# Distinct TensorE row groups for ScalarE's score sets, and a planner that serialises score matmuls sharing one

## The chip, the cores and the metric

The kernel runs on one core of a Trainium2 chip. The core has TensorE (PE in the profile; its weight loads are PEld), ScalarE (ACT), VectorE (DVE), GpSimd (POOL) and SyncE (SP), which issues the DMAs. The metric is the device time of one execution in microseconds.

## What is computed

The input x is 2048 tokens of 512 numbers. Four residual layers follow one another, A, B, A, B. A is softmax attention with 32 heads of 16 numbers that all share one key and one value head; B is linear attention with 32 heads of 16.

```python
def _A_ref(x, wq, wk, wv, wo):
    ...
    k = x @ wk
    v = x @ wv
    scores = jnp.einsum("bhqd,bkd->bhqk", q, k) * (Dh ** -0.5)
    p = _softmax(scores, axis=-1)
    o = jnp.einsum("bhqk,bkd->bhqd", p, v)
    return o.transpose(0, 2, 1, 3).reshape(B, S, H * Dh) @ wo
...
def _B_ref(x, wqkv, wo):
    ...
    pq, pk = phi(q), phi(k)
    kv = jnp.einsum("bhsd,bhse->bhde", pk, v)
    z = jnp.einsum("bhsd->bhd", pk)
    num = jnp.einsum("bhqd,bhde->bhqe", pq, kv)
    den = jnp.einsum("bhqd,bhd->bhq", pq, z)[..., None] + 1e-6
    return (num / den).transpose(0, 2, 1, 3).reshape(B, S, D) @ wo
...
x = x + _A_ref(_layernorm(x, axis=-1), A_wq, A_wk, A_wv, A_wo)
x = x + _B_ref(_layernorm(x, axis=-1), B_wqkv, B_wo)
x = x + _A_ref(_layernorm(x, axis=-1), A_wq, A_wk, A_wv, A_wo)
x = x + _B_ref(_layernorm(x, axis=-1), B_wqkv, B_wo)
```

## The kernel before

**The tiles.** An attention layer is cut into 32 units of 64 positions. A position is one score tile: 128 keys by 512 columns (queries of one or more heads). Its matmul contracts over 32 rows of TensorE's array (line 1035), and `parts` names which: position j of a unit uses row group i = j % 4, so neighbouring positions go 0, 1, 2, 3, 0, and so on. Matmuls in different row groups can run side by side.

**Two ways to the exponential.** A tile's exponential is made in one of two ways. ScalarE takes a *set* of three tiles (banks 0 to 2) or of two (banks 3 and 4) and turns it in one activation (line 1192) into PTA, of which there are five buffers. VectorE takes single tiles from banks 5 and 6: a first pass (line 1252, "P1" in the code) writes the exponential's bits as 16-bit whole numbers; three shifted copies per four tiles follow, on VectorE (line 1323) or in pieces on GpSimd (line 1313). The four versions are weighted in the PV matmuls, so a tile of VectorE's costs four PV matmuls and one of ScalarE's costs one. All PV matmuls (line 1072) go to 32 columns of the array each and add up in bank 7, which belongs to one unit at a time: when the unit is through, the bank is copied out (line 1084) and the next unit's PV matmuls may begin.

**The order.** No order is written out. When the program is built, `Sched` plays the kernel through with a clock of its own: every operation has a list of engines, a duration, a priority (a smaller number goes first) and buffers to acquire; whenever an engine is free, the first ready operation by priority is put on it. The order so found becomes the static instruction order of each engine, and only the waits between engines are left to the chip. TensorE has three modes in this model, scores ("S"), PV and column-tiled projections ("P"), and full-array matmuls ("F"); `pe_need` charges SWITCH between modes and keeps matmuls of one group apart. PASS, 0.217, is the planner's time of one pass. Some thirty knobs, such as HOLD, LEAD, BK, AP and the priorities PX and EVP, are changed every 6 us of the planner's clock by the table PLAN.

**Picking.** `step` (lines 1105 on) fills a free set: it walks from the first open position `pa` and takes the next positions that are not taken and whose keys and queries are ready. `fill` adds the score matmul, the exp and the PV matmuls of the set. Right after it, `dstep` picks a tile for VectorE LEAD positions ahead, in a row group that the set doesn't use where there is one. Positions that VectorE has taken are holes in what ScalarE's sets find later.

**The handover between layers.** `b_tile` finishes layer B for one token tile and prepares the next attention layer's; its operations carry priorities `pr`, from 1.0 upwards with the tile's number, as do those of `a_ready`. `layer_norm` is called with the same slope.

**Ports.** An operation with `port=True` on VectorE isn't started by the planner while GpSimd is at work, nor GpSimd's while such an operation runs (`_try`).

Of the kernel before, what the change touches and what calls it, by code (L numbers as in the profile page):

```python
# [20 lines left out]
LX = 0.338  # L21
HOLD = 0.836
# [36 lines left out]
YDT = 4  # L59
WT = 20.0  # L60
# [12 lines left out]
    (0.0, {'LX': 0.338, 'HOLD': 0.836, 'LEAD': 16, 'LEAD2': 14, 'NT0': 3, 'DMIN': 1, 'MP': 1, 'AP': 0.771, 'MF': 0.285, 'AF': 2.905, 'PCONT': 0.992, 'PX': 2.788, 'EVP': 1.5, 'EVX': 1.016, 'PQP': 1.6, 'PB': 1.6, 'PY': 4.497, 'PKV': 4.5, 'PTR': 2.887, 'PQL': 3.988, 'PHL': 3.855, 'PZ': 0.131, 'BK': 2.611, 'BKX': 0.376, 'BKR': 0.5, 'NPX': 6, 'PXP': 1.839, 'PXM': 0.376, 'PXA': 3.319}),  # L73
    (6.0, {'MF': 0.758, 'PX': 0.523, 'EVP': 0.969, 'PQP': 3.044, 'PTR': 1.57, 'PXM': 0.55, 'PXA': 4.0}),
    (12.0, {'EVP': 1.5, 'EVX': 1.666, 'PY': 3.366, 'PXM': 0.658}),
    (18.0, {'LX': 0.165, 'LEAD2': 15, 'NT0': 5, 'AP': 1.43, 'PX': 1.03, 'EVP': 0.969, 'EVX': 1.016, 'PY': 4.497, 'PXM': 0.55}),
    (24.0, {}),
    (30.0, {}),
    (36.0, {}),
    (42.0, {}),  # L80
    (48.0, {'PXM': 0.477}),
    (54.0, {'PKV': 3.114, 'PXM': 0.55, 'PXA': 3.298}),
    (60.0, {'LX': 0, 'MF': 0.453, 'EVP': 1.3, 'PQP': 2.524, 'PKV': 4.5, 'BKR': 0.271, 'PXM': 0.509, 'PXA': 4.0}),
    (66.0, {'HOLD': 0.625, 'LEAD2': 13, 'PQP': 2.757, 'PQL': 4.333, 'PXM': 0.51, 'PXA': 3.279}),
    (72.0, {'LX': 0.165, 'HOLD': 0.836, 'LEAD2': 15, 'AP': 2.013, 'MF': 0.758, 'EVP': 0.969, 'PQP': 3.044, 'PQL': 3.988, 'BKR': 0.5, 'PXM': 0.477, 'PXA': 4.0}),
    (78.0, {}),
    (84.0, {'AP': 0.235, 'EVX': 0.926, 'PQL': 4.305, 'BKR': 0.06, 'NPX': 5, 'PXM': 0.55}),
    (90.0, {'AF': 0.264, 'EVP': 0.5, 'PB': 1.661}),
    (96.0, {'AP': 1.43, 'AF': 2.905, 'PCONT': 0.519, 'EVP': 0.637, 'EVX': 1.016, 'PB': 1.6, 'PKV': 3.114, 'PQL': 4.602, 'BKR': 0.5, 'NPX': 6, 'PXA': 5.495}),
    (102.0, {'LX': 0.299, 'LEAD2': 14, 'PCONT': 0.64, 'BK': 5.514}),  # L90
    (108.0, {'LX': 0.165, 'LEAD2': 15, 'AP': 2.013, 'PCONT': 0.992, 'EVP': 1.815, 'PQP': 3.261, 'PKV': 4.5, 'PQL': 3.988, 'BK': 2.611, 'PXM': 0.477, 'PXA': 4.0}),
    (114.0, {}),
    (120.0, {'DMIN': 2}),
    (126.0, {'DMIN': 1, 'MP': 7, 'AP': 0.235, 'AF': 0.264, 'EVP': 0.5, 'EVX': 0.926, 'PQP': 3.044, 'PB': 1.661, 'PQL': 4.305, 'BKR': 0.06, 'NPX': 5, 'PXM': 0.55}),
    (132.0, {'LEAD2': 14, 'NT0': 3, 'DMIN': 2, 'MP': 1, 'AF': 2.905, 'EVP': 0.969, 'PB': 1.6, 'BKX': 1.173}),
    (138.0, {'HOLD': 0.825, 'NPX': 4, 'PXM': 0.32}),
    (144.0, {'HOLD': 0.836, 'LEAD2': 15, 'NT0': 5, 'AP': 2.013, 'AF': 2.795, 'EVP': 1.815, 'EVX': 1.173, 'PQP': 3.261, 'PQL': 3.988, 'BK': 3.918, 'BKX': 0.376, 'BKR': 0.5, 'NPX': 6, 'PXM': 0.477}),
    (150.0, {'AP': 0.738, 'BK': 0.896}),
    (156.0, {'HOLD': 0.651}),
    (162.0, {'PX': 3.422, 'PTR': 0.919}),  # L100
    (168.0, {'HOLD': 0.836, 'MP': 3, 'AP': 2.035, 'MF': 0.722, 'PCONT': 1.248, 'PX': 1.03, 'PQP': 1.861, 'PY': 4.5, 'PTR': 1.57, 'BK': 3.918}),
    (174.0, {'BKR': 1.227, 'PXM': 0.29}),
    (180.0, {'MP': 2, 'PCONT': 1.789, 'PQP': 3.771, 'PY': 1.858, 'PXP': 2.121, 'PXA': 3.431}),
    (186.0, {'DMIN': 1, 'EVP': 2.0}),
    (192.0, {'HOLD': 0.641, 'DMIN': 2}),
    (198.0, {}),
    (204.0, {'LEAD': 18, 'NPX': 1}),
    (210.0, {'LEAD': 16, 'EVP': 1.273, 'PTR': 1.665, 'PZ': 0.1, 'NPX': 6, 'PXP': 1.498}),
    (216.0, {'MP': 1, 'AF': 0.584, 'EVP': 2.0, 'PTR': 1.57, 'PZ': 0.131, 'BKX': 0.186, 'PXP': 2.121}),
    (222.0, {'LEAD': 18, 'AP': 1.138, 'PX': 1.994, 'PQL': 3.517}),  # L110
    (228.0, {}),
    (234.0, {'PKV': 3.786, 'PXA': 4.241}),
    (240.0, {'LX': 0.338, 'HOLD': 0.836, 'LEAD': 16, 'LEAD2': 14, 'NT0': 4, 'DMIN': 1, 'AP': 0.771, 'MF': 0.758, 'AF': 2.905, 'PCONT': 0.992, 'PX': 0.523, 'EVP': 1.5, 'EVX': 1.016, 'PQP': 3.287, 'PY': 4.497, 'PKV': 4.5, 'PQL': 3.988, 'BK': 2.611, 'BKX': 0.376, 'BKR': 0.5, 'PXP': 1.839, 'PXM': 0.645, 'PXA': 4.0}),
    (246.0, {}),
    (252.0, {}),
    (258.0, {'LEAD': 17, 'PB': 1.821, 'PTR': 1.458, 'PHL': 2.076, 'NPX': 9}),
    (264.0, {}),
    (270.0, {'LX': 0.165, 'HOLD': 0.641, 'LEAD': 18, 'LEAD2': 15, 'NT0': 5, 'DMIN': 2, 'AP': 2.993, 'MF': 0.722, 'AF': 0.584, 'PCONT': 1.789, 'PX': 1.994, 'EVP': 2.0, 'EVX': 0.948, 'PQP': 3.771, 'PB': 1.6, 'PY': 1.858, 'PKV': 3.297, 'PTR': 1.57, 'PQL': 3.517, 'PHL': 3.855, 'BK': 3.918, 'BKX': 0.186, 'BKR': 1.227, 'NPX': 6, 'PXP': 2.121, 'PXM': 0.29, 'PXA': 4.241}),
    (276.0, {}),
    (282.0, {'LX': 0.338, 'HOLD': 0.836, 'LEAD': 16, 'LEAD2': 14, 'NT0': 4, 'DMIN': 1, 'AP': 0.771, 'MF': 0.758, 'AF': 2.905, 'PCONT': 0.992, 'PX': 0.523, 'EVP': 1.5, 'EVX': 1.016, 'PQP': 3.287, 'PY': 4.497, 'PKV': 3.022, 'PQL': 3.988, 'BK': 1.481, 'BKX': 0.686, 'BKR': 0.5, 'PXP': 1.839, 'PXM': 0.645, 'PXA': 4.0}),  # L120
    (288.0, {'NT0': 3, 'DMIN': 2, 'MP': 2, 'EVX': 2.307, 'PQP': 3.044, 'PY': 4.5, 'PKV': 4.5, 'BK': 2.611, 'BKX': 0.376, 'PXM': 0.55}),
    (294.0, {}),
    (300.0, {'MP': 1, 'MF': 0.675, 'AF': 2.071, 'EVX': 1.496, 'PY': 4.497, 'BKX': 0.863, 'BKR': 0.871}),
    (306.0, {'LX': 0.321, 'HOLD': 0.641, 'LEAD': 18, 'LEAD2': 15, 'NT0': 5, 'AP': 2.993, 'MF': 0.722, 'AF': 0.584, 'PCONT': 1.789, 'PX': 1.994, 'EVP': 2.0, 'EVX': 0.948, 'PQP': 3.771, 'PY': 1.858, 'PKV': 3.297, 'PQL': 3.517, 'BK': 3.918, 'BKX': 0.186, 'BKR': 1.227, 'PXP': 2.121, 'PXM': 0.29, 'PXA': 4.241}),
    (312.0, {'LX': 0.331, 'HOLD': 0.48, 'LEAD2': 24, 'EVX': 1.448, 'PZ': 0.16}),
    (318.0, {'HOLD': 0.507, 'PXA': 3.973}),
    (324.0, {'EVX': 2.238, 'PXA': 1.205}),
    (330.0, {'LX': 0.321, 'HOLD': 0.641, 'LEAD2': 15, 'DMIN': 1, 'PX': 1.201, 'EVX': 0.948, 'PQL': 2.158, 'PHL': 1.07, 'PZ': 0.1, 'PXM': 0.298, 'PXA': 4.241}),
    (336.0, {'MF': 0.51, 'PCONT': 0.63, 'BKX': 0.274, 'PXP': 3.076}),
    (342.0, {'NT0': 3, 'EVP': 2.297, 'PTR': 1.732, 'PZ': 0.546, 'BKR': 1.5, 'PXM': 0.385}),  # L130
    (348.0, {'MF': 0.184}),
    (354.0, {}),
    (360.0, {'NT0': 5, 'MF': 0.722, 'PCONT': 1.789, 'EVP': 1.821, 'EVX': 0.573, 'PTR': 1.57, 'PZ': 0.1, 'BKX': 0.186, 'BKR': 1.227, 'PXP': 2.121, 'PXM': 0.298, 'PXA': 5.082}),
    (366.0, {'NT0': 2, 'PX': 3.845}),
    (372.0, {'LX': 0.338, 'HOLD': 0.836, 'LEAD': 16, 'LEAD2': 14, 'NT0': 3, 'AP': 0.771, 'MF': 0.758, 'AF': 2.905, 'PCONT': 0.992, 'PX': 0.523, 'EVP': 1.5, 'EVX': 1.016, 'PQP': 3.044, 'PY': 4.497, 'PKV': 4.5, 'PTR': 2.242, 'PQL': 3.988, 'PHL': 3.855, 'PZ': 0.131, 'BK': 2.611, 'BKX': 0.376, 'BKR': 0.5, 'PXP': 1.839, 'PXM': 0.355, 'PXA': 3.748}),
    (378.0, {'LEAD': 15, 'PB': 1.926, 'NPX': 4}),
    (384.0, {'NT0': 5, 'AF': 2.802, 'EVX': 2.838, 'PB': 1.6, 'BKR': 0.361, 'PXM': 0.364}),
    (390.0, {}),
    (396.0, {'DMIN': 2, 'AP': 1.529, 'PX': 3.842, 'PHL': 0.984, 'PXP': 0.75}),
    (402.0, {}),  # L140
    (408.0, {'EVP': 1.664, 'PQP': 3.211, 'NPX': 1}),
    (414.0, {'LEAD2': 15, 'PTR': 0.969, 'PQL': 1.195, 'NPX': 2, 'PXP': 1.756}),
    (420.0, {'EVX': 1.801, 'PQL': 1.84, 'PHL': 1.27, 'PXA': 2.587}),
    (426.0, {'HOLD': 0.841, 'LEAD2': 13, 'PY': 3.549, 'BKX': 0.607}),
    (432.0, {}),
    (438.0, {}),
    (444.0, {}),
    (450.0, {'HOLD': 0.836, 'LEAD2': 9, 'NT0': 3, 'DMIN': 1, 'AP': 0.771, 'AF': 2.905, 'PX': 0.523, 'EVP': 1.5, 'EVX': 1.589, 'PQP': 3.044, 'PY': 4.497, 'PTR': 1.313, 'PQL': 3.988, 'PHL': 3.855, 'BK': 2.321, 'BKX': 0.376, 'BKR': 0.5, 'NPX': 6, 'PXP': 1.839, 'PXM': 0.55, 'PXA': 4.0}),
# [6 lines left out]
    (492.0, {}),  # L155
    (498.0, {}),
    (504.0, {}),
    (510.0, {'LEAD': 12, 'EVX': 1.95, 'PQL': 3.343, 'BKX': 0.579}),
    (516.0, {}),
    (522.0, {}),  # L160
    (528.0, {}),
# [1497 lines left out]
```

## Time and profile before

| what | value |
|---|---|
| median of 3 runs (range) | 1495.05 us (1494.92 to 1497.63) |
| the profiled execution | 1498.8 us |
| its span | 1497.1 us |
| PE busy | 1459.2 us (97%), 16245 matmuls |
| ACT busy | 1444.9 us (97%), 1426 instructions |
| DVE busy | 1376.5 us (92%), 2433 instructions |
| POOL busy | 853.2 us (57%), 1360 instructions |
| exps of the first attention layer | 13.4 to 713.2 us |
| exps of the second attention layer | 749.7 us to 1456.2 us (start of the last) |

Every sum below is made against the span of the profiled execution. A busy PE is not PE at its peak, since several small matmuls can share the array at once. In the rows of groups, the part behind the first bar is the busy time in microseconds and the mean of one instruction in nanoseconds; behind the second bar stands how long the engine had been idle just before them, and what ended that idle time. In a row of the timeline stand the start, the length, the engine, the line and how many instructions were merged.

### The profile page before, as it was taken

The numbers are of one execution on the slowest core, as the hardware profiler recorded it, in microseconds if no ns is written. First come the engines' busy times: TensorE is split into PE (matmuls) and PEld (weight loads), VectorE is DVE, ScalarE is ACT, GpSimd is POOL, SyncE is SP. The second block draws the span as 40 slices with busy tenths as digits, with TensorE's granted clock in tenths as the row PEclk, the third lists the DMA queues.
The fourth block names the chain that finished last, engine by engine and source line by source line (L and its number), as shares of the span: only waits on it lengthen the run. The fifth ranks groups of instructions, "written<-read, shape, count | busy, mean of one in ns | idle before, by whom it ended". The sixth has DMA issues, their size and how long they took to land.

```text
span 1497.1 us, 38261 instructions
## 1 busy us (share of the span) xinstructions
PE 1459.2 (97%) x16245; PEld 492.0 (33%) x16255; DVE 1376.5 (92%) x2433; ACT 1444.9 (97%) x1426; POOL 853.2 (57%) x1360
## 2 busy tenths in 40 slices
PE   7999999999999999999899999999999999999998
PEld 4322333322333333333442333333333232333334
DVE  7999998999988999899798999989999899989987
ACT  7999999999999999999698999999999999999996
POOL 3556656565563655565544556566565456565654
PEclk9999999999999999999998999999999999999999
DMA  3000000000000000000000000000000000000001
GB/s 118 26 9 5 9 12 5 5 5 4 14 6 7 5 5 17 9 8 9 2 1 5 5 9 8 9 5 5 5 5 15 6 5 5 9 16 8 6 9 57
DMA packets 46251, 17.71 MB, mean 12 GB/s; under 512 B 39936, under 2 KB 45568, under 8 KB 46080
## 3 DMA queue, kind: packets, MB, share of 16 engines
q1 hardware_dynamic: 46080, 15.27, 4.3%
q8 instruction: 127, 2.08, 0.6%
q14 instruction: 44, 0.36, 0.1%
HBM read 5.28 MB, written 2.10 MB: 5 GB/s over the span
## 4 chain that ended last, share of the span: by engine, by line
PE 58%; ACT 23%; DVE 19%; issue 1%; POOL 0%; DMA 0%; SPq 0%; ACTq 0%
PE ps_all L1072 24%; PE ps_all L1035 23%; ACT PTA L1192 20%; DVE PTD L1252 10%; PE ps_all L768 7%; DVE PTD L1323 5%; PE ps_all L772 2%; PE ps_all L1093 2%; DVE Eo L1084 1%; DVE stats L840 1%; ACT e_buf L1576 1%; ACT e_buf L1439 1%; ACT e_buf L1577 1%; DVE e_buf L1446 0%; DVE x_sb L1431 0%
## 5 line engine op out<-in xcount | busy, mean ns | idle before, releaser
L1192 ACT ACTIVATE PTA<-ps_all 128x1536 bf16<-128x1536 f32 (+1 forms) x1178 | 1357.8, 1292 | 18.7 <-PE ps_all L1035 15.0
L1313 POOL TENSOR_SCALAR PTD<-PTD 128x512 uint16<-128x512 uint16 x1124 | 683.2, 618 | 489.2 <-DVE PTD L1323 317.6
L1252 DVE TENSOR_SCALAR PTD<-ps_all 128x512 uint16<-128x512 f32 x1142 | 751.1, 680 | 69.9 <-PE ps_all L1035 65.4
L1035 PE MATMUL ps_all<-QT,Kr 32*128 32x512 bf16 x4141 | 658.6, 385 | 9.9 <-ACT PTA L1192 3.6
L1072 PE MATMUL ps_all<-PTD,Vaug 128*32 128x512 bf16 x4568 | 616.2, 386 | 5.8 <-DVE Eo L1084 5.2
L1072 PE MATMUL ps_all<-PTA,Vaug 128*32 128x512 bf16 x2954 | 533.8, 387 | 0.2
L1323 DVE TENSOR_SCALAR PTD<-PTD 128x2048 uint16<-128x2048 uint16 x577 | 403.6, 711 | 2.2
L1035 PEld LDWEIGHTS ps_all<-QT,Kr 32*128 32x128 bf16 x4141 | 169.1, 91 | 493.0 <-ACT PTA L1192 220.1
L1072 PEld LDWEIGHTS ps_all<-PTD,Vaug 128*32 128x32 bf16 x4568 | 158.6, 94 | 218.1 <-issue 141.5
L1072 PEld LDWEIGHTS ps_all<-PTA,Vaug 128*32 128x32 bf16 x2954 | 131.8, 94 | 145.8 <-issue 114.2
L768 PE MATMUL ps_all<-wqkv_sb,xnT 128*32 128x512 bf16 x960 | 72.5, 382 | 0.1
L1448 POOL TENSOR_SCALAR e_buf<-e_buf 128x512 f32<-128x512 f32 x60 | 36.8, 613 | 43.1 <-ACT e_buf L1439 23.9
L1446 DVE TENSOR_SCALAR e_buf<-ps_all 128x512 f32<-128x512 f32 x60 | 40.9, 685 | 14.3 <-ACT e_buf L1439 14.2
L1439 ACT ACTIVATE e_buf<-ps_all 128x512 f32<-128x512 f32 x64 | 41.7, 655 | 9.7 <-PE ps_all L772 6.5
L1450 POOL TENSOR_TENSOR pqT<-e_buf 128x512 bf16<-128x512 f32 x30 | 38.0, 1268 | 11.8 <-DVE PTD L1323 8.0
L1450 POOL TENSOR_TENSOR pk_tok<-e_buf 128x512 bf16<-128x512 f32 x30 | 38.1, 1272 | 10.5 <-DVE PTD L1323 9.4
L1084 DVE COPY Eo<-ps_all 128x512 f32<-128x512 f32 x62 | 42.3, 682 | 1.5 <-PE ps_all L1072 1.3
L840 DVE BATCH_NORM_STATS2 stats<-x_sb 128x6 f32<-128x512 bf16 x64 | 42.9, 678 | 0.5 <-DMA x_sb<-in_A_x_dram 0.2
L1093 PE MATMUL ps_all<-identf,Eo 128*128 128x128 f32 x256 | 42.4, 289 | 0.0
L768 PE MATMUL ps_all<-wo_sb,OT 128*32 128x512 bf16 x480 | 37.7, 382 | 0.0
L1578 POOL TENSOR_TENSOR pqT<-pqT,e_buf 128x512 bf16<-128x512 bf16 x20 | 23.2, 1164 | 25.1 <-ACT e_buf L1577 6.5
L929 POOL TENSOR_SCALAR Vaug<-Vaug 128x32 bf16<-128x32 bf16 x48 | 14.9, 311 | 32.1 <-DVE Vaug L925 15.5
(102 smaller groups left out, 686.2 us busy)
## 6 DMA issues: line engine op xcount, KB each, us to landing
out_dram<-x_sb SPq DMA_DIRECT2D x16, 128.0 KB, 1.7
OT<-Osb SPq DMA_TRANSPOSE x120, 2.4
xnT<-xn_buf SPq DMA_TRANSPOSE x120, 2.3
wqkv_sb<-in_B_wqkv_dram SPq DMA_DIRECT2D x4, 384.0 KB, 3.1
x_sb<-in_A_x_dram SPq DMA_DIRECT2D x3, 256.0 KB, 3.4
x_sb<-in_A_x_dram SPq DMA_DIRECT2D x1, 768.0 KB, 7.9
wq_sb<-in_A_wq_dram SPq DMA_DIRECT2D x1, 512.0 KB, 6.4
x_sb<-in_A_x_dram SPq DMA_DIRECT2D x1, 512.0 KB, 8.7
```

What stands on the lines that cost most here:

```text
L768: i = e.matmul(out[32 * c:32 * c + 32], lhsT=lhsT[:, 32 * c:32 * c + 32], rhs=rhs, start=start, stop=stop, skip_group_check=True)
L840: add(DV, tdv(512), lambda e: e.bn_stats(stats[:, t, 0:6], x_sb[:, t, :]), reads=[("x", t)], writes=[("st", t)], prio=prio, name="bn")
L1035: x = e.matmul(bank(b0 + k), lhsT=Kr[r, m, kt * P:(kt + 1) * P], rhs=QT[r, self.units[u][0] % 2, gs, q0:q0 + n], start=True, stop=True)
L1072: return e.matmul(ps[32 * c:32 * c + 32, 7 * 512:8 * 512], lhsT=Vaug[:, kt, r, :], rhs=src() if callable(src) else src, start=opened[0], s ...
L1084: return (e.copy if oe.eng == AC else e.tensor_copy)(Eo[:, he.idx, :], bank(7))
L1093: i = e.transpose(bank(ht.idx, P, qs * P), Eo[:, he.idx, qs * P:(qs + 1) * P], identf[:])
L1192: oe = add(AC, tac(m * 512), lambda e: e.activation(PTA[:, hp.idx, 0:m * 512], bank(SETS[s][0], m * 512), ACTF.Exp, scale=SCALE), deps=[o] ...
L1252: o = add(DV, tdv(512), lambda e: e.tensor_scalar(out=PTD[:, hp.idx, i * 512:(i + 1) * 512], in0=bank(db), scalar1=SCALE * LOG2E * 128.0, ...
L1313: return e.tensor_scalar(out=PTD[:, ht.idx, i * 512:(i + 1) * 512], in0=PTD[:, hp.idx, i * 512:(i + 1) * 512], scalar1=float(SHIFT[r]), sc ...
L1323: return e.tensor_scalar(out=PTD[:, ht.idx, 0:512 * m], in0=PTD[:, hp.idx, 0:512 * m], scalar1=float(SHIFT[r]), op0=ALU.add, **kw)
L1439: o1 = add(AC, tac(512), lambda e: e.activation(e_buf[:, he.idx, :], bank(h.idx), ACTF.Exp), deps=[o], uses=[h], acq=[he] if fast else [he ...
L1450: add(PO, PHS, lambda e: e.tensor_tensor(out=dst, in0=sh(e_buf[:, hr.idx, :]), in1=sh(e_buf[:, he.idx, :]), op=ALU.add), deps=[o2, o3], us ...
```

## The change

Three things are changed in the code, and the table PLAN is new.

First, the pick for a set. A position whose row group the set already has is put aside, if it lies within DJ = 16 places of `pa`; the walk goes on to later positions. Only when too few distinct ones are found is the set filled from those put aside.

```diff
-                got, p = [], self.pa
+                got, p, used, left = [], self.pa, set(), []
                 while p < n and len(got) < w:
                     if not self.taken[p]:
-                        if not self.ok(p):
+                        if self.pos[p][2] in used and p < self.pa + DJ:
+                            left.append(p)
+                        elif not self.ok(p):
                             break
-                        got.append(p)
+                        else:
+                            got.append(p)
+                            used.add(self.pos[p][2])
                     p += 1
+                got += [q for q in left[:w - len(got)] if self.ok(q)]
```

Second, the duration of a set's score matmuls in the planner: one PASS for each matmul in the fullest row group, instead of one for up to four matmuls.

```diff
-            o = add(PE, PASS * (-(-m * RG // P)) * (2 if twice else 1), f, ...
+            rows = [self.parts(q)[0] for q in got]
+            o = add(PE, PASS * max(rows.count(i) for i in rows) * (2 if twice else 1), f, ...
```

Third, new constants: PBL = 0.04 (a port operation of VectorE is held back that much longer behind GpSimd in the planner), PSL = 0.06 (the slope of the priorities in the handover, 0.02 before; the first layer keeps 0.02 in `a_ready`), PSO = 1.0 and R0 = 0.

```diff
-            if e == DV and o.port and self.tfree[PO] > self.now + 1e-9 or e == PO and self.dport > self.now + 1e-9:
+            if e == DV and o.port and self.tfree[PO] > 0.0 and self.tfree[PO] + PBL > self.now + 1e-9 or e == PO and self.dport > self.now + 1e-9:
...
+        if e == PO:
+            self.at(end + PBL, None)
...
-                    pv = self.add_pv(p, lambda src=src, i=i: ..., src, dep[0 if r and not split else i], r, 1)
+                    pv = self.add_pv(p, lambda src=src, i=i: ..., src, c["p1"][-1] if R0 and not r else dep[0 if r and not split else i], r, 1)
...
     def b_tile(L, t, nxt):
-        pr = 1.0 + 0.02 * t
+        pr = 1.0 + PSL * t
...
-        ... name="den", prio=pr - 0.4 ...
+        ... name="den", prio=pr - 0.4 * PSO ...
...
-                layer_norm(t, 1.0 + 0.02 * t, lambda o3: a_ready(nxt, t), win)
+                layer_norm(t, 1.0 + PSL * t, lambda o3: a_ready(nxt, t), win)
...
     def a_ready(L, t):
-        pr = 1.0 + 0.02 * t
+        pr = 1.0 + (PSL if L else 0.02) * t
```

In PLAN, 214 rows have other values. Two of them, as they are before and after:

```diff
-    (12.0, {'EVP': 1.5, 'EVX': 1.666, 'PY': 3.366, 'PXM': 0.658}),
+    (12.0, {'NT0': 3, 'DMIN': 1, 'AP': 0.771, 'MF': 0.514, 'PCONT': 0.113, 'PX': 0.523, 'EVP': 1.5, 'EVX': 1.016, 'PB': 1.6, 'PTR': 1.57, 'PQL': 3.988, 'PXM': 0.434}),
...
-    (24.0, {}),
+    (24.0, {'NT0': 5}),
```

## The prediction

> **What bounds the kernel now.** I read the groups of instructions first, for who works how long, then the windows of the steady stretch, then the waits, then the chain, and last single matmuls on the timeline. The groups give the two engines that empty the score banks:
>
> ```profile
> L1192 ACT ACTIVATE PTA<-ps_all 128x1536 bf16<-128x1536 f32 (+1 forms) x1178 | 1357.8, 1292 | 18.7 <-PE ps_all L1035 15.0
> L1252 DVE TENSOR_SCALAR PTD<-ps_all 128x512 uint16<-128x512 f32 x1142 | 751.1, 680 | 69.9 <-PE ps_all L1035 65.4
> L1035 PE MATMUL ps_all<-QT,Kr 32*128 32x512 bf16 x4141 | 658.6, 385 | 9.9 <-ACT PTA L1192 3.6
> L1323 DVE TENSOR_SCALAR PTD<-PTD 128x2048 uint16<-128x2048 uint16 x577 | 403.6, 711 | 2.2
> ```
>
> There are 4096 score tiles of 128x512. VectorE takes 1142, ScalarE the other 2954. For ScalarE one tile costs 1357.8 / 2954 = 0.46 us; for VectorE it costs (751.1 + 403.6) / 1142 = 1.01 us, the shifts of line 1323 included. The last column is the point: ScalarE idled 15.0 us for a score matmul, VectorE 65.4 us. The window from 200 to 400 us (columns PE, PEld, DVE, ACT, POOL, granted clock, DMA share, GB/s) shows the same in a steady stretch:
>
> ```profile
> 200.00:400.00 200.00, 196.95 (x2180) 62.44 (x2176) 187.16 (x321) 198.39 (x178) 115.82 (x185) 1.00 0.03 7
> ```
>
> ScalarE is busy 99% of it. So time can be won only if ScalarE's few waits go, or if VectorE, busy 94%, takes tiles from it; each microsecond that VectorE gets back is 1/1.01 tile, worth 0.46 us of ScalarE. The chain of waits says who decides when they are fed:
>
> ```profile
> PE 58%; ACT 23%; DVE 19%; issue 1%; POOL 0%; DMA 0%; SPq 0%; ACTq 0%
> PE ps_all L1072 24%; PE ps_all L1035 23%; ACT PTA L1192 20%; DVE PTD L1252 10%; PE ps_all L768 7%; DVE PTD L1323 5%; PE ps_all L772 2%; PE ps_all L1093 2%; DVE Eo L1084 1%; DVE stats L840 1%; ACT e_buf L1576 1%; ACT e_buf L1439 1%; ACT e_buf L1577 1%; DVE e_buf L1446 0%; DVE x_sb L1431 0%
> ```
>
> TensorE holds more of it than both emptying engines, and score matmuls alone have 23%. Two neighbouring score stretches on the timeline show what the change is about:
>
> ```profile
> 402.12 0.60 PE L1035 MATMUL ps_all<-QT,Kr 32*128 32x512 bf16 x3
> ...
> 402.98 0.39 PE L1035 MATMUL ps_all<-QT,Kr 32*128 32x512 bf16 x3
> ```
>
> Both are three matmuls of 0.38 us. The second stretch lasts 0.39: the three start 3 to 4 ns apart and run side by side in different row groups. The first lasts 0.60: its third matmul starts 0.22 us after the second, as one that waits for its row group must. I call 0.22 us one **pass**.
>
> **The pick (line 1131 and after).** Listing every score matmul by its start and cutting the list where a semaphore is raised, I count 95 ScalarE sets of two or three whose last matmul starts 0.15 to 0.6 us behind the first. Some records are missing, so 95 is nearer a floor. Distinct row groups remove one pass each: 95 x 0.22 = 20.9 us of TensorE. No instruction is added: the same 4096 tiles, the same exps, PV matmuls and DMAs.
>
> How much of the 20.9 lies on the path? Lower end: of all exps and first passes that idled for a score matmul, those within 1.3 us behind one of the 95 idled 3.6 us on ScalarE (12 exps) and 5.7 us on VectorE (12). That is 3.6 + 5.7 / 1.01 x 0.46 = 6.2 us. Below zero is not excluded, because the order of everything else changes; it has its own case below. Upper end: all of both waits goes, 15.0 + 65.4 / 1.01 x 0.46 = 44.8 us. The nearest row is the chain: 23% of 1497.1 = 344 us of score matmuls lie on it, out of 658.6 us busy, so 52% of a score microsecond is on the path. 20.9 x 0.52 = **10.9 us**, which I take. What is late next is again VectorE behind line 1035, since most of its 65.4 us followed no such set.
>
> A rule of the Trainium skill speaks against this: TensorEngine Tiling (Array Packing), section PSUM Bottleneck, says that tiling speeds up TensorE and not the emptying of PSUM, which may then bound. By the rule, with ScalarE at 99%, only its own 3.6 us counts and the median falls to about 1491. By the rows, VectorE, one of the two emptying engines, stands idle 65.4 us for scores, so a faster array does feed the emptying. I go by the rows and keep 1491 as a rival.
>
> **The model of the matmul's duration (line 1185).** The planner's clock charged 0.217 us to any set; it now charges as many passes as the fullest row group needs. No instruction results; the static order follows the hardware more closely where a collision stays. With the sets distinct it speaks seldom: 0, held between -1 and +1 us (a tenth of the 10.9 either way, my choice).
>
> **PBL.** VectorE's port operations are planned 0.04 us later behind GpSimd. What GpSimd can cost VectorE here is bounded by the shifts of line 1323: their excess over the fast ones (676 ns) sums to 22.2 us, with only 25 of 577 over by a tenth. The delay is only in the model; in the chip it permutes. Between a gain of 22.2 / 1.01 x 0.46 = 10 us and a loss of 577 x 0.04 = 23 us of VectorE, or 10 us of ScalarE, I take 0: most of the excess is ordinary scatter, not a blocked port.
>
> **PSL, and 214 rewritten rows of PLAN.** PSO = 1.0 multiplies by one and R0 = 0 keeps the old dependence: no effect. PSL orders the second block's token tiles more steeply (priority 1.0 to 1.9 where it was 1.0 to 1.3), against fixed priorities such as 1.5 for evictions. It acts in the handover, 713 to 750 us, where no exp of attention runs: ScalarE is busy 25.53 of 37, so 11.5 us is the most it could win. As much could be lost. The trace cannot say which, nor can it for the plan's knobs: each permutes the order of existing work. I take 0 and keep +-11.5 us.
>
> **The clock.** The cores' one weak spot in the middle is this:
>
> ```profile
> 800.00:820.00 20.00, 19.52 (x160) 5.44 (x157) 17.04 (x29) 16.71 (x15) 10.78 (x18) 0.83 0.02 3
> 820.00:840.00 20.00, 19.79 (x182) 5.39 (x178) 16.94 (x28) 17.25 (x16) 10.90 (x18) 0.83 0.03 6
> 840.00:860.00 20.00, 19.86 (x214) 6.09 (x213) 20.00 (x38) 20.00 (x19) 12.22 (x21) 1.00 0.04 8
> ```
>
> The granted clock was 0.5 from 813.0 to 826.7 us; ScalarE was busy 33.96 of these first 40 us and 20.00 of the next 20, so the stretch cost 6.0 us. The skill's page TensorE: Matmul & The Clock Gate (What's actually happening) lets the clock drop after an idle window of some 3.4 us. By that rule no drop is due here, for TensorE was busy 19.52 of 20 us; by the row a sparse array is enough (160 matmuls where the third window has 214). So a new order can move it. Fewer passes for the same matmuls leave the array no emptier in sum. I leave one such stretch in the forecast: 0, between -6 (none) and +6 (two).
>
> **Sum.** 1497.1 - 10.9 = 1486.2 us of span. The profiled execution took 1498.8 us, 1.7 over its span; the median of the runs is 1495.05, 2.05 under that span. 1486.2 - 2.05 = **1484 us**, -0.7%.
>
> **Rivals.** *The passes were hidden anyway:* ScalarE is the bound, and only its 3.6 us come back: 1491. For it: ScalarE at 99%, and just 30 waits over it in the whole span. Against it: VectorE's 65.4 us.
>
> *The sets still collide:* VectorE has taken the tiles that would fill a set, the distinct search finds none within 16 places and the leftovers fill the set: 1495. Against it: VectorE takes one tile in 3.6, and 16 places hold each row group four times before that.
>
> *Slower, a jam at the unit's end:* a set may now pick over the border of a unit of 64 tiles. A PV of the next unit must wait until bank 7 is copied out (line 1084), and meanwhile its set holds one of the five PTA buffers. If every one of 64 borders cost ScalarE what TensorE's PV loads wait there now (21.5 us in 48 waits, 0.45 us each), that is 28.8 us: 1484 + 29 = 1513. It decides above 10.9 / 64 = 0.17 us a border. Against it: the five buffers hold about 5 x 1.15 us of exps, and no exp waits for a PV today.
>
> *The rewritten order loses:* handover and clock go the wrong way together, +11.5 and +6 on the forecast: 1501.5.
>
> **How the numbers follow.** Forecast 0.56, with a range of its own of 1474 to 1491; hidden 0.13; still colliding 0.06; jam 0.13; order 0.12. About 0.2% (3 us) is what a measurement of this kernel tells from no change. Faster: 0.54 of the forecast and 0.08 of the hidden case, 0.62. Same: 0.02, 0.05 and 0.05, so 0.12. Slower: the last two and a hundredth, 0.26. The range goes down by 11.5 + 6 from 1484, to 1466, and up by the same to 1502; PBL's 10 us either way are not stacked on top, since both ends at once are unlikely and 17.5 holds them alone. It leaves out the jam and a little of the forecast's lower end.
>
> **What would show it.** Right: nearly no set of 0.60 us with three matmuls; VectorE's idle before line 1252 under 60 us; more than 1142 first passes and fewer than 2954 tiles for ScalarE, by ten to twenty. Wrong: exps that wait for PV or PTA at unit borders; a second stretch at half clock; a handover longer than 36 us between the exps of the two attention blocks; or VectorE's share falling, which would lengthen ScalarE's work by 0.46 us a tile.

## The result: 1487 us, 0.6% less

The changed kernel takes 1486.8 us (median of a second series of four), the kernel before 1494.9: a ratio of 0.994 with a 95% interval of 0.9923 to 0.9957. Of the first series, three executions took 1486.1 to 1487.6 us and the profiled one 2322 us, with TensorE slower from end to end for a reason that its trace does not show (its score matmuls took 506 ns in the median, against 384 at full clock and 602 to 604 in the stretches at half clock); what follows uses a second profiled execution, with a span of 1484.6 us in a run of 1486.6.

The profiled execution of before that the prediction used (1498.8 us) was itself above its median of 1494.9. So the kernel before was profiled a second time: span 1494.3 us, run 1496.1. I compare 1484.6 with 1494.3: 9.7 us. First the rows of groups of that second execution of before (busy and mean, then idle time ahead and what ended it):

```profile
L1192 ACT ACTIVATE PTA<-ps_all 128x1536 bf16<-128x1536 f32 (+1 forms) x1178 | 1357.3, 1292 | 13.9 <-PE ps_all L1035 10.4
...
L1252 DVE TENSOR_SCALAR PTD<-ps_all 128x512 uint16<-128x512 f32 x1142 | 750.1, 679 | 65.9 <-PE ps_all L1035 61.3
...
L1035 PE MATMUL ps_all<-QT,Kr 32*128 32x512 bf16 x4141 | 656.7, 383 | 9.9 <-ACT PTA L1192 3.6
```

And the changed kernel:

```profile
L1205 ACT ACTIVATE PTA<-ps_all 128x1536 bf16<-128x1536 f32 (+1 forms) x1182 | 1356.2, 1337 | 4.6 <-PE ps_all L1042 3.5
...
L1265 DVE TENSOR_SCALAR PTD<-ps_all 128x512 uint16<-128x512 f32 x1132 | 743.7, 679 | 65.4 <-PE ps_all L1042 61.0
...
L1042 PE MATMUL ps_all<-QT,Kr 32*128 32x512 bf16 x4144 | 632.6, 384 | 11.2 <-ACT PTA L1205 5.4
```

ScalarE's idle time ahead of its exps fell from 13.9 to 4.6 us: 9.3 us, nearly the whole difference of the spans. Its exps were busy no longer than before (1356.2 us, 1357.3 before), though they took ten tiles more; the section on the prediction says how. VectorE's idle time ahead of its first pass did not move (65.9 and 65.4), and VectorE took fewer tiles, 1132 and not 1142. The score matmuls' busy time fell by 24 us for nearly the same number of matmuls. The prediction took the rest of the work to be the same; it is not quite: 7492 PV matmuls where there were 7522, since a tile of VectorE's costs four of them, and 116 transposing DMAs of xn_buf for 120. What these are worth was not measured. The chain of waits has changed its owner:

```profile
ACT 66%; PE 27%; DVE 5%; POOL 1%; issue 1%; DMA 0%; POOLq 0%; SPq 0%; ACTq 0%
ACT PTA L1205 64%; PE ps_all L1079 10%; PE ps_all L1042 9%; PE ps_all L775 4%; PE ps_all L779 3%; DVE PTD L1265 1%; ACT e_buf L1452 1%; PE ps_all L1100 1%; DVE PTD L1336 1%; POOL pqT L1591 1%; DVE stats L847 1%; PE ps_all L878 0%; ACT e_buf L1589 0%; DVE e_buf L1459 0%; DVE xn_buf L866 0%
```

Before, TensorE held 58% in both profiled executions, ScalarE 22 or 23%. Now ScalarE holds two thirds: it is fed so well that its own work ends last. The windows (columns PE, PEld, DVE, ACT, POOL, granted clock, DMA share, GB/s) show it for the two attention layers. In the second execution of before, ScalarE is busy 655.11 and 632.77 us of them:

```profile
40.00:700.00 660.00, 651.38 (x7268) 207.52 (x7265) 616.60 (x1059) 655.11 (x589) 385.58 (x611) 1.00 0.04 9
...
780.00:1420.00 640.00, 634.46 (x7101) 201.84 (x7099) 604.14 (x1041) 632.77 (x571) 374.59 (x592) 1.00 0.04 7
```

In the changed kernel it is busy 99.7% and 99.6% of them:

```profile
40.00:700.00 660.00, 652.52 (x7271) 210.16 (x7269) 616.75 (x1069) 658.03 (x595) 392.01 (x623) 1.00 0.04 9
...
780.00:1420.00 640.00, 631.63 (x7097) 202.19 (x7093) 596.16 (x1026) 637.46 (x578) 374.64 (x594) 1.00 0.04 8
```

The handover between the attention layers gave nothing: 37.5 us without an exp in the second execution of before, 38.4 now.

Grouping score matmuls whose starts lie within 0.1 us gives about 2000 passes before and 1862 after, some 137 fewer. In the built programs, 127 of 1178 sets shared a row group before (107 of the sets of three, 20 of the sets of two), and none of 1182 after. It follows that the second part of the change does nothing here: with all sets distinct, the new formula for the duration always yields one PASS, and the program without it is the same.

### The profile page after: what moved, and what is told of

Read it like the earlier page. It is cut to its first block, busy times and chain, and to the rows that moved or that the text cites. A ratio compares the mean times of both kernels' runs of the same rounds, so it can differ in the third digit from the quotient of the medians.

```text
span 2320.2 us, 37960 instructions
## 1 busy us (share of the span) xinstructions
PE 2307.0 (99%) x16108; PEld 534.4 (23%) x16108; DVE 1418.3 (61%) x2406; ACT 1551.0 (67%) x1436; POOL 867.1 (37%) x1364
## 4 chain that ended last, share of the span: by engine, by line
PE 99%; DVE 1%; DMA 0%; ACT 0%; issue 0%
PE ps_all L1079 43%; PE ps_all L1042 33%; PE ps_all L775 12%; PE ps_all L779 7%; PE ps_all L1100 3%; PE ps_all L878 1%; PE ps_all L1389 0%; DVE Eo L1091 0%; DVE stats L847 0%; DMA x_sb<-in_A_x_dram 0%; DVE PTD L1265 0%; DVE xn_buf L866 0%; DVE xnT L884 0%; DVE Kr L911 0%; ACT e_buf L1452 0%
## 5 line engine op out<-in xcount | busy, mean ns | idle before, releaser
L1205 ACT ACTIVATE PTA<-ps_all 128x1536 bf16<-128x1536 f32 (+1 forms) x1182 | 1447.8, 1239 | 649.8 <-PE ps_all L1042 648.1
L1079 PE MATMUL ps_all<-PTD,Vaug 128*32 128x512 bf16 x4528 | 986.6, 609 | 1.5 <-DVE Eo L1091 1.4
L1042 PE MATMUL ps_all<-QT,Kr 32*128 32x512 bf16 x4144 | 861.0, 549 | 0.3 <-DVE PTD L1265 0.3
L1079 PE MATMUL ps_all<-PTA,Vaug 128*32 128x512 bf16 x2964 | 836.3, 583 | 0.0
L1336 DVE TENSOR_SCALAR PTD<-PTD 128x2048 uint16<-128x2048 uint16 (+1 forms) x571 | 387.3, 689 | 2.0
L1042 PEld LDWEIGHTS ps_all<-QT,Kr 32*128 32x128 bf16 x4144 | 132.7, 93 | 868.0 <-issue 501.8
L775 PE MATMUL ps_all<-wqkv_sb,xnT 128*32 128x512 bf16 x928 | 138.2, 632 | 0.0
L779 PE MATMUL ps_all<-Msb,pqT 128*128 128x512 bf16 x128 | 63.9, 678 | 0.0
L775 PE MATMUL ps_all<-xnT,wq_sb 128*32 128x512 bf16 x384 | 56.9, 632 | 0.0
L775 PE MATMUL ps_all<-xnT,wqkv_sb 128*32 128x128 bf16 (+1 forms) x576 | 46.9, 447 | 0.0
```

The costliest lines, as they stand in the source:

```text
L775: i = e.matmul(out[32 * c:32 * c + 32], lhsT=lhsT[:, 32 * c:32 * c + 32], rhs=rhs, start=start, stop=stop, skip_group_check=True)
L779: return e.matmul(out, lhsT=lhsT, rhs=rhs, start=start, stop=stop, skip_group_check=True)
L1042: x = e.matmul(bank(b0 + k), lhsT=Kr[r, m, kt * P:(kt + 1) * P], rhs=QT[r, self.units[u][0] % 2, gs, q0:q0 + n], start=True, stop=True)
L1079: return e.matmul(ps[32 * c:32 * c + 32, 7 * 512:8 * 512], lhsT=Vaug[:, kt, r, :], rhs=src() if callable(src) else src, start=opened[0], s ...
L1205: oe = add(AC, tac(m * 512), lambda e: e.activation(PTA[:, hp.idx, 0:m * 512], bank(SETS[s][0], m * 512), ACTF.Exp, scale=SCALE), deps=[o] ...
L1336: return e.tensor_scalar(out=PTD[:, ht.idx, 0:512 * m], in0=PTD[:, hp.idx, 0:512 * m], scalar1=float(SHIFT[r]), op0=ALU.add, **kw)
```

## The experiments

Theory A is the forecast's mechanism, the passes saved. Theory B says that the rewritten table and the handover bring the gain. Theories C and D came up on the way. Times are medians; each ratio is to runs of the kernel before in the same series.

**The changed kernel again.** No edit.

> The changed kernel once more, for a trace at full clock[...]. Both theories: 1487 us, within 2. Theory A (the passes saved shorten the waits for scores): VectorE's idle before its first pass on a tile falls from 69.9 us to under 60, ScalarE's idle before its exps from 18.7 to about 15, and no set of three takes 0.60 us. Theory B (the new table of knobs brings the gain, above all in the handover between the attention layers): these two idle times stay within 5 us of before, and the 36.4 us between the exps of the two layers, or the stretch at half clock from 813 to 826.7 us, shrink by 6 us or more.

1486.8 us. ScalarE's wait fell by more than theory A said; VectorE's did not fall, against it. Of theory B's signs, neither the two idle times as a pair nor the handover fit; the stretch at half clock turned out to be a matter of the execution (see below).

**The kernel before again.** No edit.

> The kernel before once more, for a second trace: its first profiled execution took 4 us more than its median. If the stretch at half clock (813 to 826.7 us) made these 4 us, it is missing here, the span is 1492 to 1494 us and ScalarE's idle before its exps falls from 18.7 to 13 or 14 us. If the stretch belongs to the order of the kernel, all is as before.

The span is 1494.3 us (0.3 above the range) and ScalarE's idle time ahead of its exps 13.9, as expected of a stretch that comes and goes. It is the trace that the changed kernel's has to be held against.

**The new pick alone, and everything but the new table.**

```diff
 # b_pick: before, with
+    the new walk over positions (used, left), DJ = 16
 # a_oldplan: after, with
-PLAN = (the 245 rows of after)
+PLAN = (the 245 rows of before)
```

> The kernel before with the new pick alone (old durations, old table, old slope). Its program has no set with a shared row group, where the kernel before has 127. Theory A: 1484 to 1489 us, most of the gain. Theory B: 1493 us or more, since the old table was made for another order; slower than before is possible.

> The changed kernel with the old table of knobs; pick, durations, PBL and PSL as changed. Theory A: 1485 to 1491 us. Theory B: at or above the 1495 us of before.

1536.5 us (ratio 1.029, 1.0243 to 1.0337) and 1559.4 us (1.0426, 1.041 to 1.0443). Theory A missed by 47 and 68 us. The bounds of theory B hold, but it had named no loss of this size. Every set has distinct row groups in both, and both are far slower. The pick alone shows where it goes:

```profile
L1198 ACT ACTIVATE PTA<-ps_all 128x1024 bf16<-128x1024 f32 (+1 forms) x1171 | 1355.5, 1289 | 55.1 <-PE ps_all L1036 52.1
...
L1258 DVE TENSOR_SCALAR PTD<-ps_all 128x512 uint16<-128x512 f32 x1150 | 756.7, 680 | 95.8 <-PE ps_all L1036 91.0
```

ScalarE now idles 55.1 us ahead of its exps, 52.1 of them for scores: four times as long as before. This cannot be the price of shared sets, for there are none. So either distinct sets do harm, or any order but the one the table was made with is slow. The next runs tell these apart.

**An edit without a meaning.** The planner's time of a transposing DMA, in the kernel before and in the changed one:

```diff
-TDI = 5.1
+TDI = 5.15
```

> The kernel before with the planner's time of a transposing DMA at 5.15 us in place of 5.1: no meaning of its own, only another order under the same table. Theory C (the table fits the one order that it was made with): 1520 to 1560 us, as the two runs with the old table and another order had (1536, 1559). If those two were slow because distinct row groups do harm, this one stays at 1490 to 1500.

> The changed kernel with the same meaningless edit. Theory C: 1510 to 1550 us, so slower than the unchanged kernel although every set still has distinct row groups. If the pick carries the gain by itself: 1484 to 1492.

Before with the edit: 1574.0 us (1.053, 1.0488 to 1.0572), slower than with the pick, though the rule of picking was not changed and 114 sets share a row group. It lies 14 us above the range of theory C. Distinct sets are thus not needed for such a loss: another order under the old table is enough, as theory C has it. The changed kernel with the edit: 1498.0 us (1.0011, 1.0001 to 1.002), outside what C said. The trace tells why. In each of the first thirteen hundreds of microseconds ScalarE's idle time ahead of its exps is the unchanged kernel's within 0.1 us; only what lies behind differs:

```profile
1300.00:1400.00 100.00, 99.00 (x1195) 32.66 (x1191) 88.77 (x156) 95.30 (x88) 57.52 (x89) 1.00 0.06 12
```

The unchanged kernel there:

```profile
1300.00:1400.00 100.00, 98.54 (x1235) 33.58 (x1234) 92.18 (x162) 99.89 (x93) 58.66 (x91) 1.00 0.05 11
```

ScalarE is busy 95.30 us of the hundred, not 99.89. The edit took hold late: the first 1051 of ScalarE's sets are the same in both programs. Only the last part lost its fit, and that alone cost about 11 us. As a test of C for the new table it was too weak, hence the next one.

```diff
 # a_pbl_3: after, with
-PBL = 0.04
+PBL = 0.03
```

> The changed kernel with PBL 0.03 in place of 0.04, which is almost no change in meaning, but gives another order from early on (1140 tiles for VectorE, not 1132). Theory C: 1515 to 1560 us under the new table, though no set shares a row group. If the new table holds for any order with the new pick: 1484 to 1495.

1550.9 us (1.0383, 1.0355 to 1.041). A hundredth of a microsecond in one of the planner's delays costs 64 us, with distinct sets throughout and the new table. ScalarE idles 60.5 us ahead of its exps. Theory C holds for both tables. It also means that PBL's own worth can't be read from this run, nor PSL's from a run of that kind; neither was settled.

**The passes put back, order kept.** Since every change of order costs tens of microseconds, the passes had to be changed with the order held. In the changed kernel, every ninth set issues its last score matmul twice; the planner is not told.

```diff
+            self.nset = getattr(self, "nset", 0) + 1
+            again = self.nset % 9 == 0
...
             def f(e):
+                if again:
+                    self.smm(e, got[-1:], SETS[s][0] + m - 1)
```

> The changed kernel in which every ninth set of ScalarE, 131 of 1182, issues its last score matmul twice, so that the second one waits for its row group as a colliding one did; the planner does not know of it and the order stays the same. 131 x 0.22 = 29 us of TensorE. Theory A, by the 52% of the chain: +15 us, about 1502. Theory B (the passes are hidden): +4 us or less, about 1490.

1495.2 us (0.9997, 0.9987 to 1.0006): +8.3 us for 131 doubled matmuls, 0.064 us each, between the two theories. They put the changed kernel back on the time of before:

```profile
L1210 ACT ACTIVATE PTA<-ps_all 128x1536 bf16<-128x1536 f32 (+1 forms) x1182 | 1358.6, 1293 | 8.1 <-PE ps_all L1042 5.4
...
L1270 DVE TENSOR_SCALAR PTD<-ps_all 128x512 uint16<-128x512 f32 x1132 | 745.1, 680 | 70.6 <-PE ps_all L1042 65.5
```

Both engines wait a little longer, ScalarE by 3.5 us and VectorE by 5.2. The score matmuls are busy 649.4 us, 16.8 more, and not the 29 that were expected: 0.13 us for each doubled one.

**The passes taken out, order kept.** In the kernel before, the 127 score matmuls that share a row group with an earlier one of their set are left out; those tiles are not computed.

```diff
-        def smm(self, e, ps_, b0):
+        def smm(self, e, ps_, b0, out=()):
             for k, p in enumerate(ps_):
+                if k in out:
+                    continue
...
-                return self.smm(e, got, SETS[s][0])
+                js_ = [self.pos[q][2] for q in got]
+                return self.smm(e, got, SETS[s][0], [k for k in range(m) if js_[k] in js_[:k]])
```

> The kernel before in its own order, without the 127 score matmuls that share a row group with an earlier one of their set: those 127 tiles are left out of the computation (their exps read what the bank held). It has the passes that the change removes taken out, and nothing else moved. Theory A, at the 0.064 us a pass that the doubled matmuls cost (8.3 / 131): 127 x 0.064 = 8 us, 1487. The forecast's 52% of a pass: 14.5 us, 1480. Theory B (the gain comes from the new order and the table): 1492 or more.

1485.6 us, a ratio of 0.9932 (0.9916 to 0.9949); the change's own is 0.994 (0.9923 to 0.9957). The idle times:

```profile
L1195 ACT ACTIVATE PTA<-ps_all 128x1536 bf16<-128x1536 f32 (+1 forms) x1178 | 1353.9, 1321 | 8.7 <-PE ps_all L1037 7.6
...
L1255 DVE TENSOR_SCALAR PTD<-ps_all 128x512 uint16<-128x512 f32 x1142 | 749.0, 679 | 58.7 <-PE ps_all L1037 55.5
...
L1037 PE MATMUL ps_all<-QT,Kr 32*128 32x512 bf16 x4014 | 640.0, 384 | 11.3 <-ACT PTA L1195 5.0
```

ScalarE's idle time is down to 8.7 us, VectorE's to 58.7, and the score matmuls are busy 16.7 us less than in the second execution of before. With the old order and the old table, taking the passes out gives what the change gives. This kernel also has 127 matmuls fewer, so it is a bound for the change rather than a copy of it. Its score passes fell by about 90 and not 127 (to 1910), probably because VectorE's tile often ran in the same second pass and still needs one. With about 10 us gained (the interval is 7.6 to 12.6) that is 0.08 us for each matmul left out.

**The pick where nothing is fitted.** An empty table leaves the knobs at their starting values, so that old and new pick, and old and new duration, meet on equal terms.

```diff
-PLAN = (245 rows)
+PLAN = ()
```

> The kernel before with an empty table: the knobs keep their starting values throughout, so its order was fitted to nothing. 108 sets share a row group. Theory C (a table fits one order): near the other unfitted orders, 1530 to 1580 us. It is the base for the next two.

> The same with the new pick: no shared set. Theory A, at 0.06 to 0.10 us for each of 108 passes: 7 to 11 us under the empty table's time with the old pick. If distinct row groups only help a fitted order: no difference, or one of either sign beyond 20 us, as large as the orders differ among themselves.

> The kernel before with an empty table and the old pick, but with the new durations: the planner knows of the second pass of each of its 130 shared sets. Theory D (what hurt was that the planner didn't know): most of the new pick's gain, so within 4 us of the time with the new pick. Theory A (the passes themselves cost): no gain over the old durations, beyond what another order does.

| empty table with | shared sets | median us | ratio to before (interval) |
|---|---|---|---|
| old pick, old duration | 108 | 1552.5 | 1.0398 (1.0368 to 1.0428) |
| new pick | 0 | 1538.9 | 1.0297 (1.0282 to 1.0313) |
| old pick, new duration | 130 | 1554.8 | 1.0421 (1.0374 to 1.0469) |

By these medians the pick is worth 13.6 us, but the clock is in them: the mean granted clock was 0.988 to 0.998 in the executions with the old pick, 0.986 to 0.998 in those with the new durations, and 0.998 in all four with the new pick. The executions at 0.997 or 0.998 took 1550.2 and 1551.1 us (old pick), 1547.8 and 1548.5 (new durations), and 1538.6 to 1539.9 (new pick). At like clock the pick is thus worth 11 to 12 us, and that the planner knows of the second pass 2 to 3. Theory D falls, since it wanted the new durations within 4 us of the new pick and they are 8 to 10 away: the passes have to go. The rows of the old pick, of the new durations and of the new pick, all under the empty table:

```profile
L946 ACT ACTIVATE PTA<-ps_all 128x1536 bf16<-128x1536 f32 (+1 forms) x1198 | 1385.6, 1281 | 45.7 <-PE ps_all L789 42.4
...
L1006 DVE TENSOR_SCALAR PTD<-ps_all 128x512 uint16<-128x512 f32 x1084 | 719.8, 685 | 155.3 <-PE ps_all L789 149.1
```

```profile
L947 ACT ACTIVATE PTA<-ps_all 128x1536 bf16<-128x1536 f32 (+1 forms) x1199 | 1384.8, 1275 | 33.2 <-PE ps_all L789 28.8
...
L1007 DVE TENSOR_SCALAR PTD<-ps_all 128x512 uint16<-128x512 f32 x1087 | 720.3, 684 | 141.1 <-PE ps_all L789 136.1
```

```profile
L952 ACT ACTIVATE PTA<-ps_all 128x1536 bf16<-128x1536 f32 (+1 forms) x1203 | 1383.6, 1310 | 29.6 <-PE ps_all L790 28.1
...
L1012 DVE TENSOR_SCALAR PTD<-ps_all 128x512 uint16<-128x512 f32 x1076 | 714.2, 684 | 155.3 <-PE ps_all L790 149.7
```

From the old pick to the new one ScalarE's idle time falls, 45.7 to 29.6 us, and VectorE's stays, but this is no reading of the pick: the trace with the old pick has two stretches at half clock, 294.0 to 307.7 and 543.2 to 560.3 us, in and just behind which ScalarE idled 13.0 of its 45.7 us. The trace with the new durations had the clock of the one with the new pick (0.998), and 130 shared sets; against it ScalarE's idle time is only 3.6 us shorter, and VectorE's is longer. So the times speak for the pick, but which engine's wait it shortens can't be read here. One pair of orders is thin evidence where orders differ by tens of microseconds; it stands beside the two runs that kept the order.

## Why the prediction was right, and where it wasn't

**The mechanism** was right. Distinct row groups took out score passes, and the passes are the gain: with the order kept, taking them out of the old order gave a ratio of 0.9932, and doubling 131 score matmuls in the new order cost 8.3 us, against 8.1 us of the change.

**The sum** was 95 passes of 0.22 us, of which 52% count, 10.9 us; measured are 8.1. Two of its factors were mis-sized, in opposite directions. The count: 127 sets collided, not 95; nor was 95 a floor made of collisions alone, for the same test still finds 33 sets in the trace of the changed kernel, where no set shares a row group (8 of them of three tiles, 57 before). The size: leaving out the 127 matmuls took 16.7 us off the busy time of the score matmuls, doubling 131 added 16.8, so a collision costs TensorE 0.13 us of busy time and not 0.22. The share of 52%, taken from the chain, held: about 10.2 of those 16.7 us came off the time (61%; 46 to 75% over the interval) and 8.3 of the 16.8 came on (49%). In the change itself, where the order differs too, it is 8.1 of 24.1 us (34%). That the errors of count and size nearly cancel is luck.

**The way the gain would take** was wrong. The forecast gave VectorE's 65.4 us of waiting the larger part and looked for ten to twenty more tiles there. VectorE's wait stayed and it took ten fewer tiles; that and a handover of 38.4 us are two of the signs that the prediction had named as wrong. The time came out near the forecast all the same because ScalarE's own idle time fell, from 13.9 to 4.6 us. That, too, is luck.

What the prediction left out is that a wait costs ScalarE more than its idle time. In the trace of the second execution of before, an exp of three tiles that starts behind an idle gap takes 1451 ns of ScalarE's time, one that follows directly on the instruction before it 1344 (medians, counted from the end of that instruction); for two tiles they are 1024 and 916. So each start from a standstill costs 0.107 us on top of the gap. 80 of 1178 exps started so before, 35 with the passes left out and 24 of 1182 in the changed kernel. In the change that is 6.0 us won beside the 9.3 of idle time, against 4.3 us for the ten tiles more (0.43 us each).

The lower end of the forecast, 3.6 us on ScalarE, was well read as far as it went. With the order kept, exp can be held against exp: those of the 127 colliding sets idled 3.65 us in the second execution of before and 0.16 with the passes left out. But they also took 3.9 us less of ScalarE's time once they started, and the other 1051 exps gained 3.0 us in both together: 10.4 us in sum, where the spans differ by 11.6. So most of the cost stood at the colliding sets themselves. With the matmuls doubled it was about half: 3.9 us at the sets that had one, 4.3 at the others. Why VectorE's wait stays in the change, though it fell by 7.2 us where the order was kept, was not settled. Nor is it known which part of ScalarE's 9.3 us belongs to the passes and which to the new order and table: 5.2 us went with the passes alone.

**The rule** on the emptying of PSUM, weighed in the prediction, gave 1491 and the rows 1484; 1487 lies midway. It was right in that VectorE took no more work, wrong in that ScalarE, the busiest of the engines that empty, still had waits to lose.

**The table** was priced at 0 within 11.5 us either way. Its net price, together with the new order, is near 0: the passes account for the change within the few microseconds by which these runs can tell. But the bound was taken from the handover's idle time, which is the wrong row. Without its new rows the changed kernel takes 1559 us, so the table gives 73 us; 64 of them only make good what the new order loses under the old table. The trace of before could not show this, and the forecast should have said that a pick that alters every later choice can cost more under the old table than the passes bring.

**The new durations** were priced at 0 and change no instruction, as said above. **PBL and PSL** stay open: the one trial, of PBL, made another order, and PSL was not tried by itself. Of PSL it can be said that the handover did not shorten (37.5 to 38.4 us).

**The clock** was priced at 0 for one stretch staying. The stretch from 813 to 826.7 us belonged to one execution, not to the kernel: in the second it is gone, ScalarE's idle time ahead of exps between 800 and 900 us is 1.5 us where it was 6.3, and the span 2.8 us shorter. Part of the wait that the prediction counted on, 15.0 us for scores, was therefore the clock's; 10.4 us is the figure of the second execution.

**The rivals:** *hidden* fell with the two runs that kept the order; *still colliding* with the count of zero; the *jam* did not come, since 38 sets cross a unit's border both before and after, and no exp is seen to wait for a PV; *the order loses* came true under the old table, though by 41 and 64 us and as waits for scores all along the kernel, not in the handover and the clock; the new table averted it.

## What to carry to other kernels

Where small matmuls run side by side in row groups, look in the timeline for a group that lasts a pass longer than its neighbours, and choose its members so that they differ: removing the collision helped more than telling the planner of it (11 to 12 us against 2 to 3, in one pair of orders). A static order fitted by a table holds only for the order it was fitted to: a meaningless edit cost 5% here, so a change to any early choice must be measured with the order kept (issue the work twice, or leave it out), or on an unfitted base. The chain's share of a line (52% here) was a fair guide to what a microsecond of its busy time is worth (49 and 61%), but that microsecond has to be measured: a pass of 0.22 us on the timeline was 0.13 us of busy time. And count how often the busiest engine starts from a standstill, not only how long it stands.

## What the runs showed of the hardware

The stretches at half clock move between executions of one program: 813.0 to 826.7 us in one trace of the kernel before, 725.3 to 728.8 and 1469.4 to 1472.9 in another. Of 13 runs of that kernel in one series, the seven with a mean granted clock of 0.999 took 1494.2 to 1494.9 us, the one with 0.995 took 1499.1. A difference of 0.3% between two single executions of this kernel can thus be the clock alone. The Trainium skill's page TensorE: Matmul & The Clock Gate (What's actually happening) asks for an idle window of about 3.4 us before the clock falls; between 800 and 820 us, where the first of these stretches begins, TensorE was idle for less than 0.5 us in sum, so no such window preceded it. The 160 matmuls that the prediction read there as a sparse array prove nothing, since part of that window already ran at half clock; what made the clock fall is not shown. In the 13 traces that record the clock there are 34 such stretches. Each lasts 3.4 us or two to five times as long, and in the 7 us before one the longest unbroken idle time of TensorE was between 0.2 and 2.7 us; none reached 3.4.
